# The rounding constant of the angles as a row of the angle product: three matrix products per PSUM bank in place of four

## The chip, the cores and the metric

The kernel runs on one core of a Trainium2 chip. The metric is the device time of one execution in microseconds, given as a median of several runs. Beside it stands one profiled execution, whose trace shows every instruction of the engines: TensorE (PE in the profile, its weight loads PEld), VectorE (DVE), ScalarE (ACT), GpSimd (POOL) and SyncE (SP, which here only issues transfers).

## The reference

All data are float32. `x` has 2048 positions (L) and 512 channels (D). The reference is one block of two halves, each with a layer norm whose shift, scale and gate come from `silu(c) @ w_mod`.

```python
# first half: an S4 convolution, with N = 128 states per channel
dt = exp(log_dt)[:, None];  logdA = dt * (A_re + 1j * A_im);  dB = dt * (B_re + 1j * B_im)
P = exp(logdA[:, :, None] * l[None, None, :])               # l = 0 .. L-1
K = einsum("dn,dnl,dn->dl", C_re + 1j * C_im, P, dB).real   # one filter of length L per channel
y = irfft(rfft(K, 2L) * rfft(u, 2L))[:, :L] + u * Dskip     # causal convolution, by FFT
# second half: a dense layer of 1792, mish, a dense layer back to 512
h = layernorm(x + ga * y) * (1 + cb) + sb
out = (x + ga * y) + gb * (mish(h @ w1 + b1) @ w2)
```

What matters here is `P`: for every channel and state a complex exponential, that is a decay and an angle, at every position.

## The kernel before, in words

The work falls into three stages.

The first, up to about 250 us of the span, makes the filters and their transform. Position `l` is split into a coarse and a fine part, so that the exponentials of 16 channels (`k`, one of 32 groups) are a table of 32 by 64 per state. `params` computes logarithms and angles of the parameters in four blocks `b` of 128 channels, on VectorE. They go out to DRAM (`store_pk`) and come back transposed as stationary matrices (`load_s`): `S12` for the angles, with 96 rows, of which rows 64 to 95 are ones, and `S3` for the decays. For each group `k` there are then these steps:

- `coarse` (the `pco` products and `Exp` on ScalarE) makes the decays `co`. It is done for eight groups at a time in `visit`, between two loads of ScalarE's function tables; there are four visits.
- `s_ang(k)` makes the angles in turns. It fills a pair of PSUM banks `pang` (two per tag), each by four accumulating products with the same stationary matrix `s`: the first with `ac[:, 0]` gives the angle `a`; the second, with a column of `am` broadcast over 512 columns (stride 0), adds 12582912 (MAGIC), at which float32 has steps of one, so that the bank is rounded to whole turns; the third takes MAGIC off again; the fourth, with `ac[:, 1] = -ac[:, 0]`, takes the angle off. What stays is the rounded angle less the angle.
- `s_sin(k)` reads the pair on ScalarE three times (`Abs`, two `Sin`) and fills `ec`, of which there are three buffers.
- `s_mag(k)` and `comb(k)` multiply by the decays on VectorE, in tiles `m` and `ec`.
- `s_kgen(k)` (64 small products into `pkg`), `s_ks(k)` (the copy to `ks` on ScalarE), `s_skip(k)` (VectorE), `s_ka(k)` (16 products into `pka`) and `s_tm(k)` (the copy to `gk` on ScalarE) make the filter's first transform.

The order on each engine is written out by hand: `follow` chains every instruction of PE, ScalarE, VectorE and SP behind the one before it. In step `k` PE does `s_kgen(k-1)`, `s_ang(k+3)`, `s_ka(k-3)` and, in half of the steps, the transform of a piece of the input (`u_mm`, tile `pua`); ScalarE does `s_ks(k-1)`, `u_out`, `s_sin(k+2)`, `s_tm(k-3)`; VectorE does `comb(k)` with other pieces of work between its parts: `params` of the last block, the input's statistics (`u_stats`, tile `bst`) and norm (`u_norm`, tile `x`). Three products with rows of `w_mod` (`mod_mm`, `mod_piece`) lie in single steps. The lines for PE and for the angle product are:

```python
for s in [(s_kgen, k - 1), (s_ang, k + 3), (s_ka, k - 3)] + pe.get(k, []):
    step(*s)
for s in [(s_ks, k - 1)] + se.get(k, []) + [(s_sin, k + 2), (s_tm, k - 3)]:
    step(*s)
```

The second stage, to about 345 us, multiplies the transforms and transforms back (`product`, `inverse`, tiles `pub`, `pkb`, `y`, `pz`). The third, to the end, is the norm and the two dense layers (`pm`, `po`); products that need more precision are made of three products of split operands.

## Time and profile before

| | |
|---|---|
| median of 3 runs | 718.02 us (716.53 to 719.85) |
| the profiled execution | 714.55 us, its span 712.8 us |
| mean granted TensorE clock | 0.941 of full speed |
| PE busy | 634.3 us, 89% of the span |
| DVE busy | 412.8 us, 58% |
| ACT busy | 319.9 us, 45% |
| POOL busy | 5.0 us, 1% |

Busy time is that of an engine's instructions; those of PE are pipelined and their ends are modelled, so the distance from one start to the next is the better measure there. In rows of the timeline the columns are start, duration, engine, line, operation with output and inputs, form and count; the bracket at the end is idle time just before it and what ended it. Helpers record all operations at their own lines (L147 for most products, L119 and L141 for VectorE and ScalarE), so tiles tell more than lines.

### The profile page before, as it was taken

How to read it: one execution, taken by the hardware profiler on the slowest of the kernel's cores; microseconds unless marked ns; L12 is line 12 of the kernel's file. 1: busy time of each engine (PE TensorE's matmuls, PEld its weight loads, DVE VectorE, ACT ScalarE, POOL GpSimd, SP SyncE). 2: the span in 40 equal slices, each digit the busy share in tenths (PEclk: the TensorE clock that was granted, in tenths of full speed). 3: DMA queues.
4: the chain of work that ended last, by engine and by line, in shares of the span. 5: the costliest groups of instructions: out<-in, count | busy, mean ns of one | idle time of the engine just before them, and what ended most of it. 6: DMA issues, size and time to landing. Idle time of an engine off the chain costs nothing.

```text
span 712.8 us, 11831 instructions
## 1 busy us (share of the span) xinstructions
PE 634.3 (89%) x4848; PEld 432.8 (61%) x4848; DVE 412.8 (58%) x813; ACT 319.9 (45%) x466; POOL 5.0 (1%) x12
## 2 busy tenths in 40 slices
PE   0488899889989979999249999999999999999995
PEld 0356666556656623333028778887788867888884
DVE  8889989997976657876196242342443224441113
ACT  2477798598897644543135212322132211322220
POOL 2000000000000000000000000000000000000000
PEclk9969979879969999999669999999999999999999
DMA  7842213624342479973686140052201400020002
GB/s 194 296 135 66 90 41 111 195 74 151 118 146 93 133 202 316 307 228 131 163 240 139 37 101 0 1 119 59 60 1 29 90 0 1 1 57 4 0 1 59
DMA packets 34315, 74.63 MB, mean 105 GB/s; under 512 B 5419, under 2 KB 9903, under 8 KB 33749
## 3 DMA queue, kind: packets, MB, share of 16 engines
q1 hardware_dynamic: 33380, 72.17, 34.9%
q10 hardware_dynamic: 576, 1.05, 0.7%
q8 instruction: 38, 0.62, 0.4%
q0 software_dynamic: 304, 0.66, 0.4%
q14 instruction: 17, 0.13, 0.1%
HBM read 49.73 MB, written 24.13 MB: 104 GB/s over the span
## 4 chain that ended last, share of the span: by engine, by line
PE 69%; DVE 21%; ACT 4%; DMA 3%; issue 2%; SPq 0%; ACTq 0%; DVEq 0%
PE pm L797 22%; PE po L814 22%; DVE ec L119 8%; PE pub L147 4%; PE pz L147 4%; DVE raw L119 4%; PE pkb L147 4%; PE pang L147 3%; PE pkg L147 2%; PE pka L147 2%; PE pia L762 2%; PE pco L147 2%; DVE x L119 1%; PE pua L147 1%; ACT ec L141 1%
## 5 line engine op out<-in xcount | busy, mean ns | idle before, releaser
L797 PE MATMUL pm<-hh,w1h 128*128 128x512 f32 x448 | 142.5, 398 | 0.6 <-ACT hh L119 0.6
L141 ACT ACTIVATE mh<-pm,b 128x512 f32<-128x512 f32 x56 | 38.5, 688 | 228.2 <-PE pm L797 228.2
L119 DVE TENSOR_TENSOR mal<-mh,mah 128x512 fp32r<-128x512 f32 x56 | 38.7, 691 | 155.3 <-ACT mah L119 155.0
L797 PEld LDWEIGHTS pm<-hh,w1h 128*128 128x128 f32 x448 | 84.8, 189 | 21.6 <-ACT hh L119 1.5
L814 PE MATMUL po<-w2h,mah 128*128 128x512 f32 x224 | 89.4, 399 | 0.0
L797 PE MATMUL pm<-hh,w1l 128*128 128x512 f32 x224 | 88.7, 396 | 0.0
L814 PE MATMUL po<-w2l,mah 128*128 128x512 f32 x224 | 88.6, 395 | 0.0
L814 PE MATMUL po<-w2h,mal 128*128 128x512 f32 x224 | 88.5, 395 | 0.0
L119 DVE TENSOR_TENSOR ec<-ec,co 128x1024 f32<-128x1024 f32 x64 | 75.0, 1204 | 8.4 <-ACT ec L141 8.4
L147 PE MATMUL pang<-ac,s 96*128 96x512 f32 x128 | 53.2, 461 | 25.8 <-DMA s<-pkd 25.8
L147 PEld LDWEIGHTS pkg<-ec 128*32 128x32 f32 x2048 | 35.9, 114 | 29.4 <-issue 15.4
L119 DVE TENSOR_TENSOR y<-pkb,f 128x1024 f32<-128x1024 f32 x32 | 37.7, 1220 | 27.5 <-PE pkb L147 27.5
L814 PEld LDWEIGHTS po<-w2h,mah 128*128 128x128 f32 x224 | 42.1, 188 | 14.6 <-ACT mah L119 4.9
L147 PE MATMUL pkg<-ec 128*32 128x64 f32 x2048 | 42.0, 230 | 7.6 <-DVE ec L119 6.7
L797 PEld LDWEIGHTS pm<-hh,w1l 128*128 128x128 f32 x224 | 42.3, 189 | 10.0
L814 PEld LDWEIGHTS po<-w2h,mal 128*128 128x128 f32 x224 | 42.1, 188 | 10.2
L814 PEld LDWEIGHTS po<-w2l,mah 128*128 128x128 f32 x224 | 42.1, 188 | 9.8
L147 PEld LDWEIGHTS pang<-ac,s 96*128 96x128 f32 x128 | 27.6, 215 | 32.9 <-issue 26.3
L147 PE MATMUL pang<-am,s 96*128 96x512 f32 x128 | 43.5, 425 | 0.0
L147 PE MATMUL pco<-mc,s 64*128 64x512 f32 x64 | 30.4, 624 | 11.2 <-ACT co L141 7.1
L141 ACT ACTIVATE ec<-ec,halfpi 128x1024 f32<-128x1024 f32 x32 | 37.5, 1173 | 0.0
L147 PE MATMUL pka<-bdk,ks 128*64 128x128 f32 x512 | 36.5, 288 | 0.9 <-ACT gk L119 0.9
(97 smaller groups left out, 832.2 us busy)
## 6 DMA issues: line engine op xcount, KB each, us to landing
ud<-u SPq DMA_DIRECT2D x16, 512.0 KB, 3.4
ur<-ud SPq DMA_DIRECT2D x32, 256.0 KB, 4.3
zd<-z SPq DMA_DIRECT2D x16, 512.0 KB, 3.3
zl<-zd SPq DMA_DIRECT2D x28, 256.0 KB, 4.9
x<-in_A_u SPq DMA_DIRECT2D x32, 128.0 KB, 3.0
x<-in_A_u SPq DMA_DIRECT2D x8, 512.0 KB, 6.9
out<-ot SPq DMA_DIRECT2D x32, 128.0 KB, 2.3
w1s<-in_B_w SPq DMA_DIRECT2D x8, 448.0 KB, 6.0
```

Of the source, the lines that this page charges most:

```text
L119: ins = getattr(self.engine, name)(*a, **kw)
L141: follow("act", nc.scalar.activation(out, in_, f, **kw))
L147: follow("pe", T.matmul(out, lhsT, rhs, start=start, stop=stop))
L762: T.matmul(p[64 * tl:64 * tl + 64, :], di, ZL[tt, hv][:, j % 2, tl, :], start=True, stop=True)
L797: T.matmul(p, w1[wi][:, k, fs], hh[:, hi, k, :], start=(n == 0), stop=(n == 3 * KB - 1))
L814: T.matmul(PO[tt][q], a[ai][:, P * q:P * q + P], w2[wi][:, f, :], start=(f == 0 and n == 0), stop=(f == FB - 1 and n == 2))
```

## The change

The constant MAGIC becomes row 64 of the first angle product's moving matrix. Row 64 of the stationary matrix is ones, and rows 64 to 95 of `ac[:, 0]` were zero, so the first product now gives `a + MAGIC` at once. The product that added MAGIC is gone; `am` has one column, -MAGIC. Each bank is filled by three products in place of four; all other steps stay, in the same order.

```diff
     ac = np.zeros((2, 96, 16, 32))
-    am = np.zeros((96, 2))
+    am = np.zeros((96, 1))
...
     ac[1] = -ac[0]
-    am[64] = MAGIC, -MAGIC
+    ac[0, 64] = MAGIC
+    am[64] = -MAGIC
...
-    am = gen.tile([96, 2], F32R, name="am", bufs=1)
+    am = gen.tile([96, 1], F32R, name="am", bufs=1)
...
         for e in range(2) if half is None else (half,):
-            for n in range(4):
-                rhs = ac[:, n // 3, :] if n % 3 == 0 else am[:, n - 1:n].to_broadcast([96, 512])
-                mm(PA[k][:, e, :], s[:, e, :], rhs, start=(n == 0), stop=(n == 3))
+            for n, rhs in enumerate((ac[:, 0, :], am.to_broadcast([96, 512]), ac[:, 1, :])):
+                mm(PA[k][:, e, :], s[:, e, :], rhs, start=(n == 0), stop=(n == 2))
```

## The prediction

> **What bounds the kernel now.** I read the page first: its shares, its slices, and in the list of groups the two that the change touches.

> ```profile
> PE 634.3 (89%) x4848; PEld 432.8 (61%) x4848; DVE 412.8 (58%) x813; ACT 319.9 (45%) x466; POOL 5.0 (1%) x12
> PE   0488899889989979999249999999999999999995
> DVE  8889989997976657876196242342443224441113
> PEclk9969979879969999999669999999999999999999
> L147 PE MATMUL pang<-ac,s 96*128 96x512 f32 x128 | 53.2, 461 | 25.8 <-DMA s<-pkd 25.8
> L147 PE MATMUL pang<-am,s 96*128 96x512 f32 x128 | 43.5, 425 | 0.0
> ```

> The share of 89% says little about this change, since the angle products all lie in the first third. There (slices 2 to 13) PE and DVE are both at 8 or 9 tenths, and the granted clock dips four times. So the question is, step by step, whether PE or DVE ends last. The chain of waits over 25 to 255 us answers it: its shares, all its long pieces of `pang`, and at two places what follows them.

> ```profile
> by line: DVE ec L119 23.8%; PE pang L147 8.5%; PE pkg L147 7.5%; PE pka L147 6.5%; DVE raw L119 5.9%; PE pco L147 5.4%; issue 4.7%; PE pua L147 4.4%; ACT ec L141 3.9%; DVE x L119 3.5%; DVE bst L119 2.7%; DVE m L119 2.6%; DMA pkd<-pk 2.2%; D
> ...
> 78.26 2.00 PE pang L147 x8
> 80.26 1.02 PE pka L147 x16
> 81.28 1.06 PE pua L147 x4
> ...
> 133.69 3.42 PE pang L147 x8
> 137.11 1.91 PE pka L147 x16
> 139.01 1.97 PE pua L147 x4
> ...
> 156.85 2.50 PE pang L147 x8
> 162.53 1.99 PE pang L147 x8
> 183.45 1.99 PE pang L147 x8
> 188.89 2.00 PE pang L147 x8
> 208.84 3.71 PE pang L147 x8
> 217.35 2.00 PE pang L147 x8
> ```

> A group of eight products stands for one `s_ang`. There are 32 groups (128 + 128 products in the page's list, by 8); only eight are on the chain, 19.6 us together, which is 8.5% of 230. The others lie beside VectorE.

> **What one product costs.** The starts in PE's timeline, since durations overlap: a pair of `am` products at full clock, and one at half clock.

> ```profile
> 104.46 0.60 PE L147 MATMUL pang<-am,s 96*128 96x512 f32 x2
> 104.90 0.63 PE L147 MATMUL pang<-ac,s 96*128 96x512 f32 x2
> ...
> 135.63 1.05 PE L147 MATMUL pang<-am,s 96*128 96x512 f32 x2
> 136.47 0.63 PE L147 MATMUL pang<-ac,s 96*128 96x512 f32 x1
> ```

> At full clock 104.90 - 104.46 = 0.44 us for two, 0.22 each; at half clock 136.47 - 135.63 = 0.84. Each group loses two `am` products: a group of 2.00 us becomes 1.56, one of 3.42 becomes 2.58. Their weight loads run under the products, so I count nothing more for them. [...]

> Were every group on the path, 24 at full clock and 8 taken at half would give 24 x 0.44 + 8 x 0.84 = 17.3 us: the ceiling. If VectorE hid all, 0.

> **What is on the path.** These are the rows of PE, VectorE and ScalarE at the places where the chain changes engine.

> ```profile
> 132.03 0.27 PE L147 MATMUL pkg<-ec 128*32 128x64 f32 x2 [1.90 <-DVE ec L119]
> ...
> 81.22 0.69 DVE L119 SCALAR_TENSOR_TENSOR ec<-ec,m 128x512 f32<-128x512 f32 x1
> 139.03 0.68 DVE L119 SCALAR_TENSOR_TENSOR ec<-ec,m 128x512 f32<-128x512 f32 x1
> 166.83 1.23 DVE L119 TENSOR_TENSOR ec<-ec,co 128x1024 f32<-128x1024 f32 x1 [1.71 <-ACT ec L141]
> 170.86 0.69 DVE L119 BATCH_NORM_STATS2 bst<-x 128x6 f32<-128x512 f32 x1 [1.61 <-DMA x<-in_A_u]
> 191.17 0.69 DVE L119 SCALAR_TENSOR_TENSOR ec<-ec,m 128x512 f32<-128x512 f32 x1
> 226.84 2.33 DVE L119 TENSOR_TENSOR ec<-ec,co 128x1024 f32<-128x1024 f32 x2 [0.94 <-ACT ec L141]
> 239.96 2.33 DVE L119 TENSOR_TENSOR ec<-ec,co 128x1024 f32<-128x1024 f32 x2 [0.52 <-ACT ec L141]
> ...
> 83.49 0.37 ACT L119 COPY ks<-pkg 128x256 f32<-128x256 f32 x1 [0.49 <-PE pkg L147]
> 194.12 0.37 ACT L119 COPY ks<-pkg 128x256 f32<-128x256 f32 x1 [0.48 <-PE pkg L147]
> 236.66 0.37 ACT L119 COPY ks<-pkg 128x256 f32<-128x256 f32 x1 [1.26 <-PE pkg L147]
> ```

> I go from visit to visit, because a visit is bound by ScalarE and passes on whatever the steps before it gained.

> *To the second visit.* VectorE leads until shortly before 78, then PE runs one step without a gap to the copy at 83.49, which waits for it. The group at 78.26 is in that step: 0.44. The `kgen` behind it needs VectorE's result of 81.22 + 0.69 = 81.91, and PE would come to it at 81.28 + 1.06 - 0.44 = 81.90: VectorE is just in time. ScalarE had idled 0.49 there, so it has room for 0.44 and no more.

> *To the third visit.* VectorE is without a gap and holds PE back (1.90 us of waiting at 132.03); every group up to there is hidden and only lengthens PE's waits. Then PE does the last step at half clock: the group at 133.69 gives 0.84. What is late next is VectorE's result of 139.03 + 0.68 = 139.7; PE comes to the `kgen` behind it at 139.01 + 1.97 = 140.98, less 0.84 at 140.14, still the later of the two.

> *To the fourth visit.* PE leads first: the group of 156.85, partly at half clock, gives 0.58 (two of its eight products at 0.22 to 0.42 each lie between 0.44 and 0.84; I take the low half, since the clock comes back within it), the next one 0.44. ScalarE's result at 166.83 comes by 0.58 earlier, the input that the statistics wait 1.61 us for at 170.86 by 1.02, because its load is issued when PE's `pua` frees the buffer. 1.02 is under 1.61, so it counts in full. The group at 183.45 gives nothing: the next `kgen` starts into VectorE's end. The one at 188.89 gives 0.44: VectorE was done at 191.86, the copy at 194.12 waits for PE, and its idle 0.48 covers 0.44. Sum 1.46.

> *To the end of the stage.* The groups at 208.84 (half clock, 0.84) and 217.35 (0.44) are on the chain: 1.28, and VectorE's ec at 226.84 can follow, having idled 0.94 and, before that, longer. From there the chain names VectorE; but PE has no gap, and ScalarE's copy at 236.66 waits 1.26 for PE. Three more groups lie there, 3 x 0.44 = 1.32. So this part is worth between 1.28 (VectorE leads) and 2.60 (PE leads). VectorE's idle 0.52 at 239.96 allows 1.28 + 0.52 = 1.80; I take 1.9, near that row.

> Sum: 0.44 + 0.84 + 1.46 + 1.9 = 4.64 us. Later stages have no angle products and are moved as they are: 714.55 - 4.64 = 709.91 for an execution like the profiled one. That execution is 3.47 us under the median of 718.02, so the median forecast is 718.02 - 4.64 = 713.4.

> **Edits at no cost.** The first product gets a nonzero row; it keeps its 96 rows and 512 columns and so its time. The load of `am` shrinks; its place in POOL's queue stays, and its first reader starts at 25.8 waiting for other data. No wait is added, and nothing moves past a queue. Buffers come free sooner by at most the 4.64 us, so loads of the stationary matrices start sooner by as much; they lie ahead of need and I price them at 0.

> **The clock.** Its cost is the unknown one. These are rows of busy time in stretches of 3.41 us, aligned to the steps of the granted clock (columns: stretch, length, PE, PEld, DVE, ACT, POOL, clock, DMA share, GB/s).

> ```profile
> 69.14:72.55 3.41, 2.01 (x67) 1.71 (x68) 3.41 (x7) 1.03 (x4) 0.00 (x0) 1.00 0.28 77
> 130.58:133.99 3.41, 1.72 (x66) 1.45 (x67) 3.41 (x6) 0.47 (x2) 0.00 (x0) 1.00 0.85 234
> 133.99:137.41 3.42, 3.42 (x12) 2.31 (x12) 3.42 (x6) 3.42 (x6) 0.00 (x0) 0.50 0.55 178
> 195.43:198.85 3.42, 2.10 (x20) 1.23 (x19) 3.32 (x6) 3.40 (x6) 0.00 (x0) 1.00 0.57 214
> 198.85:202.26 3.41, 2.45 (x7) 1.05 (x7) 1.02 (x2) 3.40 (x6) 0.00 (x0) 1.00 0.00 0
> 202.26:205.67 3.41, 3.41 (x7) 1.96 (x7) 3.38 (x6) 3.41 (x8) 0.00 (x0) 0.50 0.00 0
> ```

> The clock fell to half behind a stretch with PE busy 1.72, stayed full behind ones with 2.01 and 2.10, and fell behind one of 2.45. So the limit is somewhere near 1.7 to 2.4, and a stretch where PE waits for VectorE, with 0.44 less to do, comes nearer to it. [...]

> **Rivals.**

> *VectorE covers more than the chain shows.* Its slices at 8 and 9 speak for it; the waits of ScalarE for PE (0.49, 0.48) against it. Left would be the steps just ahead of the visits, at full clock, and the group at 156.85: 0.44 + 0.44 + 0.44 + 0.58 = 1.9, so 716.1.

> *The clock falls once more.* At 69 to 72, say: a step then takes PE twice as long. The rows at 133.69 and 78.26 give the price of a step: 3.42 + 1.91 + 1.97 = 7.30 us for 2.00 + 1.02 + 1.06 = 4.08; with three products per bank 6.46 for 3.64, so 2.8. 713.4 + 2.8 = 716.2.

> *Slower: the clock falls at three new places* where PE waits for VectorE. 3 x 2.8 = 8.4, less 4.64: 3.8 us over the median, 721.8. It decides from the third fall on; two give 719.0. For it speaks that 2.01 is near the limit; against it that only that one full stretch is so near.

> *More than forecast.* The clock returns one stretch of 3.41 us earlier behind a visit (behind the last it is still at half in the group of 208.84), worth 1.7, and PE leads in four more steps, 4 x 0.44: 4.64 + 3.46 = 8.1 gives 709.9; the ceiling allows it.

> **How the numbers follow.** A measurement of this kernel can tell about 0.5%, 3.6 us, from no change. Forecast, 713.4 (its own range 711 to 714.4): 0.48. More: 0.10. VectorE covers: 0.25. One fall, or two: 0.10. Three falls: 0.07. Faster by over 0.5% is the first two, 0.58; within it the next two, 0.35; slower 0.07. The range runs from 709.5, under the case of 709.9, to 718, above the two cases near 716; three falls are left out.

> **What would show it.** `pang<-am` at 64 products, a group at 1.56 us between starts; the copies at 83.5 and 194.1 waiting under 0.1 us for PE; the input's wait at 170.9 down to about 1.2 (1.61 - 1.02 + 0.58); longer waits of PE's `pkg` for VectorE between 60 and 132; stage end about 4.6 us earlier. The prediction is wrong if half-clock stretches are more, longer or fewer than before, or if those two copies come no earlier relative to the visit before them.

## The result and the profile after

The changed kernel took 712.97 us, median of 9 runs (711.97 to 716.25), beside 717.71 for the kernel before (9 runs). The ratio is 0.995, with a 95% interval of 0.9933 to 0.9968: faster by 2.3 to 4.8 us, with 4.74 between the medians. The forecast was 713.4. The profiled execution took 711.97 us, span 710.2. It lies 1.0 us under its median and the one of before 3.2 under its own, so the two traces differ by only 2.6 us, and what is read from them is an account of these 2.6.

The page after: shares, slices and groups.

```profile
PE 623.6 (88%) x4784; PEld 422.5 (59%) x4784; DVE 412.4 (58%) x813; ACT 319.9 (45%) x466; POOL 5.0 (1%) x12
PE   0388898789889989999349999999999999999995
DVE  8979989998978577866194242322443134441113
PEclk9959978979969999999679999999999999999999
L148 PE MATMUL pang<-ac,s 96*128 96x512 f32 x128 | 56.1, 485 | 27.0 <-DMA s<-pkd 26.5
```

PE lost 10.7 us of busy time and 64 products; VectorE and ScalarE do what they did. In the slices PE shows more 7s and 8s in the first third. The clock's row has the same four dips there; its slices of 17.8 us are too coarse for what follows below. The row of the `am` products in PE's view of tile `pang`, and the ends of one group in its timeline:

```profile
L148 PE MATMUL pang<-am,s x64: 377/378/629, 27.0 to 228.8; 96*128 96x512 f32 x64
...
78.86 0.50 PE L148 MATMUL pang<-ac,s 96*128 96x512 f32 x1
...
80.43 0.33 PE L148 MATMUL pka<-bdk,ks 128*64 128x128 f32 x2
```

From 78.86 to 80.43 a group takes 1.57 us, for the 2.00 of before. Its first product, with the constant in its row 64, starts 0.34 us ahead of the next (78.86, 79.20), as in the trace of before without it (104.12, 104.46). The long pieces of `pang` on the chain of waits after:

```profile
72.97 2.78 PE pang L148 x6
78.94 1.56 PE pang L148 x6
...
156.54 2.00 PE pang L148 x6
161.72 1.55 PE pang L148 x6
...
183.73 2.07 PE pang L148 x6
188.99 1.55 PE pang L148 x6
...
208.49 2.86 PE pang L148 x6
214.89 1.56 PE pang L148 x6
219.64 1.56 PE pang L148 x6
223.33 1.56 PE pang L148 x6
227.88 1.57 PE pang L148 x6
```

Two things are new. Three groups stand behind the one at 214.89, where the chain of before named VectorE: PE leads to the end. And groups stand there at half clock (72.97, 2.78 us) or partly (183.73, 2.07) that were at full clock before. The busy time by stretches of the clock, at three places between the visits where it fell and had not fallen before:

```profile
68.68:72.09 3.41, 1.32 (x52) 0.95 (x52) 3.41 (x8) 1.61 (x3) 0.00 (x0) 1.00 0.27 77
72.09:75.50 3.41, 3.41 (x41) 2.47 (x31) 3.41 (x6) 2.49 (x4) 0.00 (x0) 0.50 0.00 0
...
109.64:113.05 3.41, 1.67 (x20) 0.99 (x18) 3.41 (x6) 3.41 (x5) 0.00 (x0) 1.00 0.81 267
113.05:116.47 3.42, 2.74 (x64) 2.48 (x65) 3.42 (x7) 0.86 (x4) 0.00 (x0) 0.50 0.03 7
...
177.91:181.32 3.41, 0.91 (x14) 0.53 (x10) 3.41 (x6) 2.79 (x4) 0.00 (x0) 1.00 0.41 156
181.32:184.73 3.41, 2.95 (x65) 2.60 (x66) 3.41 (x6) 0.92 (x2) 0.00 (x0) 0.50 0.02 5
```

Ahead of each fall VectorE was busy throughout (3.41) and PE only 1.32, 1.67 and 0.91 us: PE had finished its shorter work and waited (0.9, 1.5 and 2.1 us for VectorE's `ec`, and 1.2 for ScalarE's `gk` in the first). A fourth stretch at half clock, from 140.4 to 143.8, stands beside the one that before had from 134.0 to 140.8. So the rival of the falling clock came about in this trace, three times, and the time was still as forecast. The waits of VectorE and ScalarE after:

```profile
170.36 0.69 DVE L120 BATCH_NORM_STATS2 bst<-x 128x6 f32<-128x512 f32 x1 [1.91 <-DMA x<-in_A_u]
...
232.48 0.38 ACT L120 COPY ks<-pkg 128x256 f32<-128x256 f32 x1 [0.83 <-PE pkg L148]
```

The wait for the input at 170.36 became longer (1.61 to 1.91), not shorter. The copy at 232.48 waits 0.83 us for PE, for 1.26 before. The input's load on the two chains of waits, before and after (SP's issues, then the transfer):

```profile
166.68 0.54 SPq L446
167.27 0.74 SPq L446
168.07 2.70 DMA x<-in_A_u
```

```profile
165.43 0.55 SPq L446
166.03 0.60 SPq L446
166.68 3.58 DMA x<-in_A_u
```

Counted from the third visit, the load was issued 0.94 us sooner (19.84 to 18.90), as forecast, but had landed only 0.20 sooner (23.93 to 23.73). One of its four issues took SP 1.45 us; the longest of the same four took 0.74 before.

To see where the time went, I measure from one visit to the next, at ScalarE's first table load of each (columns: start, duration, engine, line, operation, count), and to the first `pkb` product, with which the second stage is under way. Before, then after:

```profile
35.87 1.28 ACT L144 ACT_TABLE_LOAD   x1
88.20 1.28 ACT L144 ACT_TABLE_LOAD   x1
146.84 1.28 ACT L144 ACT_TABLE_LOAD   x1
198.83 1.28 ACT L144 ACT_TABLE_LOAD   x1
253.19 3.65 PE L147 MATMUL pkb<-gk,mf 128*64 128x512 f32 x16 [1.16 <-ACT f L119]
```

```profile
36.61 1.28 ACT L145 ACT_TABLE_LOAD   x1
88.52 1.28 ACT L145 ACT_TABLE_LOAD   x1
146.53 1.28 ACT L145 ACT_TABLE_LOAD   x1
198.48 1.28 ACT L145 ACT_TABLE_LOAD   x1
249.00 3.65 PE L148 MATMUL pkb<-gk,mf 128*64 128x512 f32 x16 [1.16 <-ACT f L120]
```

The same differences, in us, for all traces but that of the added work around the visits (one execution each; the experiments follow), with the time at half clock before 250 us:

| kernel | 1 to 2 | 2 to 3 | 3 to 4 | 4 to pkb | sum | half clock |
|---|---|---|---|---|---|---|
| before | 52.33 | 58.64 | 51.99 | 54.36 | 217.32 | 54.6 |
| changed | 51.91 | 58.01 | 51.95 | 50.52 | 212.39 | 64.9 |
| changed, again | 51.79 | 57.46 | 53.69 | 49.83 | 212.77 | 64.9 |
| ten groups | 51.67 | 57.46 | 52.11 | 51.70 | 212.94 | 51.2 |
| ten groups, again | 52.10 | 57.46 | 52.49 | 50.01 | 212.06 | 51.2 |
| the 22 others | 52.42 | 57.46 | 54.17 | 51.74 | 215.79 | 64.9 |
| last five | 52.50 | 57.46 | 54.38 | 51.91 | 216.25 | 51.2 |
| first five | 52.16 | 58.13 | 51.24 | 51.47 | 213.00 | 51.2 |
| five products | 54.35 | 57.47 | 54.35 | 54.16 | 220.33 | 41.0 |
| two products | 52.88 | 57.47 | 54.05 | 49.15 | 213.55 | 71.7 |
| four waits filled | 51.50 | 58.28 | 53.27 | 49.70 | 212.75 | 58.0 |
| changed, shifted | 52.38 | 57.46 | 52.33 | 51.76 | 213.93 | 68.3 |
| ten groups, shifted | 52.11 | 58.63 | 51.45 | 49.46 | 211.65 | 51.2 |

The stage of the angles became 4.93 us shorter, but the span only 2.6. The first visit came 0.74 us later in this trace. The second stage moved as it is. The last one, from the first `pm` to the start of the last long piece of `po`, took 324.08 us before (373.14 to 697.22) and 325.63 after (369.01 to 694.64), 1.55 more. The reason is at its third set of stores. VectorE's and PE's timelines there, and the issues of the stores (least, median and most ns):

```profile
L824 SPq DMA_DIRECT2D out<-ot x32: 466/562/2025, 460.7 to 706.7; - x32
...
633.75 0.69 DVE L120 TENSOR_TENSOR ot<-po,gbb 128x512 f32<-128x512 f32 x1 [3.51 <-DMA out<-ot]
...
634.50 0.50 PE L814 MATMUL po<-w2h,mah 128*128 128x512 f32 x1 [1.07 <-DVE ot L120]
```

One store took SP 2.03 us to issue (604 ns at most before). VectorE waited 3.51 us there for an earlier store of the set to land, for 1.73 at the same place before, and PE 1.07 us for VectorE.

### The profile page after: what moved, and what is told of

Same layout as the page of the kernel before. It is cut to its first block, busy times and chain, and to the rows that moved or that the text cites. A ratio compares the mean times of both kernels' runs of the same rounds, so it can differ in the third digit from the quotient of the medians.

```text
span 710.2 us, 11704 instructions
## 1 busy us (share of the span) xinstructions
PE 623.6 (88%) x4784; PEld 422.5 (59%) x4784; DVE 412.4 (58%) x813; ACT 319.9 (45%) x466; POOL 5.0 (1%) x12
## 3 DMA queue, kind: packets, MB, share of 16 engines
q10 hardware_dynamic: 576, 1.05, 0.7%
## 4 chain that ended last, share of the span: by engine, by line
PE 70%; DVE 19%; DMA 4%; ACT 4%; issue 2%; SPq 0%; DVEq 0%; ACTq 0%
PE pm L797 22%; PE po L814 21%; DVE ec L120 6%; PE pub L148 4%; PE pz L148 4%; DVE raw L120 4%; PE pkb L148 4%; PE pkg L148 3%; PE pang L148 3%; PE pka L148 2%; PE pia L762 2%; PE pco L148 2%; DVE bst L120 2%; DVE x L120 1%; PE pua L148 1%
## 5 line engine op out<-in xcount | busy, mean ns | idle before, releaser
L148 PE MATMUL pang<-ac,s 96*128 96x512 f32 x128 | 56.1, 485 | 27.0 <-DMA s<-pkd 26.5
L148 PEld LDWEIGHTS pkg<-ec 128*32 128x32 f32 x2048 | 37.8, 119 | 32.6 <-issue 15.0
L148 PE MATMUL pkg<-ec 128*32 128x64 f32 x2048 | 43.8, 239 | 12.5 <-DVE ec L120 9.9
L814 PEld LDWEIGHTS po<-w2h,mah 128*128 128x128 f32 x224 | 42.1, 188 | 16.5 <-ACT mah L120 4.9
L148 PEld LDWEIGHTS pang<-ac,s 96*128 96x128 f32 x128 | 29.1, 228 | 36.2 <-issue 27.6
L148 PE MATMUL pz<-y,mi 64*128 64x512 f32 x128 | 32.5, 626 | 4.1 <-DVE y L120 4.1
```

The costliest lines, as they stand in the source:

```text
L148: follow("pe", T.matmul(out, lhsT, rhs, start=start, stop=stop))
L814: T.matmul(PO[tt][q], a[ai][:, P * q:P * q + P], w2[wi][:, f, :], start=(f == 0 and n == 0), stop=(f == FB - 1 and n == 2))
```

## The experiments

The theories: the gain comes from the groups that the prediction put on the path (path); every removed product gains alike (spread); and the clock takes a part back where PE waits for VectorE (clock).

**Ten groups, and the 22 others.** `am` keeps a second column, of zeros, and a product with it stands in place of the removed one in some groups:

```diff
-            for n, rhs in enumerate((ac[:, 0, :], am.to_broadcast([96, 512]), ac[:, 1, :])):
-                mm(PA[k][:, e, :], s[:, e, :], rhs, start=(n == 0), stop=(n == 2))
+            zero = [am[:, 1:2].to_broadcast([96, 512])] * (0 if k in (9, 17, 19, 20, 25, 27, 28, 29, 30, 31) else 1)
+            seq = [ac[:, 0, :], *zero, am[:, 0:1].to_broadcast([96, 512]), ac[:, 1, :]]
+            for n, rhs in enumerate(seq):
+                mm(PA[k][:, e, :], s[:, e, :], rhs, start=(n == 0), stop=(n == len(seq) - 1))
```

> Three products per bank only in ten groups, those that the prediction had on the path (k = 9, 17, 19, 20, 25, 27 to 31); in the other 22 a product with a zero column stands in the place of the removed one, so PE works there as before. 20 of 64 products are gone. If the gain comes from these groups (path theory): the whole of it, about 4.6 us under the kernel before, 713.1. If every removed product gains alike because PE leads in most steps (spread theory): 20/64 of the 4.74 us measured, 1.5, so 716.2. If falls of the clock in steps where PE waits for VectorE eat a part of the changed kernel's gain (clock theory): faster than the changed kernel by one to three falls of 1 us or more, 710 to 712, and no half-clock stretch near 72, 113 and 181 us in the trace.

Measured: 0.9915 (0.9893 to 0.9937) of the kernel before, 710.95 us. 20 of the 64 products give all of the gain, so the spread theory, which asked for 0.998, falls. The trace has no fall of the clock between the visits; the stretches that answer to the first and third of those above:

```profile
69.63:73.04 3.41, 2.74 (x69) 2.42 (x70) 3.41 (x7) 1.54 (x3) 0.00 (x0) 1.00 0.10 32
73.04:76.46 3.42, 2.76 (x24) 1.29 (x22) 3.39 (x8) 2.18 (x3) 0.00 (x0) 1.00 0.00 0
...
178.86:182.27 3.41, 2.22 (x76) 1.71 (x73) 3.41 (x8) 2.48 (x4) 0.00 (x0) 1.00 0.36 136
182.27:185.69 3.42, 3.42 (x28) 2.27 (x26) 3.42 (x5) 3.42 (x5) 0.00 (x0) 1.00 0.00 0
```

The complement (`1 if k in ... else 0`):

> The complement: three products per bank in the 22 groups beside VectorE, four (one with a zero column) in the ten others. 44 of 64 products are gone. Path theory: no gain, 717.7 within 1 us. Spread theory: 44/64 of 4.74, 3.3 us, so 714.4. Clock theory: PE idles more in the steps led by VectorE and the clock falls there, so slower than before by 1 to 3 us, 718.7 to 720.7, with new half-clock stretches near 72, 113 or 181 us.

Measured: 0.9995 (0.997 to 1.0019). No gain, with 44 of 64 products gone: the path theory. Its trace has falls at 71.1, 132.6 and 180.4 us, and half clock for 64.9 us as the changed kernel has: in this pair of traces the clock fell there where the 22 groups lacked this work, and held where they had it. The clock theory's loss of 1 to 3 us did not show; the interval leaves out over 1.4 us.

**Five products, and two.** `zero` twice in every group; and the last product left out, so that the kernel lacks the fractions of the angles:

> Two products with a zero column in each bank: five products per bank, one more than before. Path theory: at least the 4.64 us of the same groups back on the other side, 722.3, and more where hidden groups come onto the path, up to the ceiling of 17.3 us. Theory that VectorE covers nearly all: 1.9 us, 719.6. Clock theory: some of it is given back, since PE waits less for VectorE and the clock falls less often, under 4 us, 718 to 721.

Measured: 1.0038 (1.0021 to 1.0056), 719.24 us: 2.7 us for 64 more products, less than the 4.64 that the path theory asked for at least. Half clock shrank to 41.0 us, and only the visits have it. By stretch the trace lost 2.02 and 2.36 us to the second and fourth visits, won 1.17 to the third, where the clock held, and 0.20 behind the last, where it was back 12 us behind the visit and not 17. So the clock gave a part back; how much of the missing 2 us this is, one trace doesn't show.

> Leaves out the last product of each bank, which takes the angle off: two products per bank, the fractional angles are missing. Path theory: a smaller second step, since ScalarE's copies had only 0.48 us of room in the steps led by PE: 1.5 to 2.5 us under the changed kernel, 710.5 to 711.5. Spread theory: another 4.7 us, 708.3. Clock theory: PE idles still more, more half-clock stretches than in the changed kernel, and no gain over it: 713 to 716.

Measured: 0.9903 (0.9871 to 0.9936), 709.62 us: 3.3 us under the changed kernel's 712.97, between the path theory's forecast and the spread theory's. The interval is 707.5 to 712.2 us on this comparison's kernel before (716.76) and holds both, so this run decides nothing between them. Half clock rose to 71.7 us. Over the four kernels with one count in every bank it goes with the products per bank: 41.0 at five, 54.6 at four, 64.9 at three, 71.7 at two.

**The changed kernel and the ten groups once more, side by side, and four waits filled.** The third has the zero product only in groups 7, 13 and 23, and two in 16:

```diff
-            zero = [...] * (0 if k in (9, 17, 19, 20, 25, 27, 28, 29, 30, 31) else 1)
+            zero = [...] * ({7: 1, 13: 1, 16: 2, 23: 1}.get(k, 0))
```

> The changed kernel once more, beside the next three on one chip. Its first measurement was 0.995 of the kernel before. Path theory with luck of the clock's phase: 0.995 again, and half-clock stretches between the visits at other places or none in this trace. Clock theory: stretches again near 72, 113, 140 and 181 us, since they follow PE's waits for VectorE, whatever the phase.

Measured: 0.9933 (0.9911 to 0.9955). Falls between the visits at 70.7, 132.2 and 179.9 us, as the clock theory said, but none at 113: the places are those of PE's waits, and which of them loses the clock varies.

> Three products per bank in the ten groups on the path, four in the 22 others, beside the changed kernel on the same chip. Clock theory: 1.5 to 3 us under the changed kernel, as 0.9915 against 0.995, and no half-clock stretch between the visits. If the difference was the chip or the draw: equal to the changed kernel within 1 us.

Measured: 0.9908 (0.9885 to 0.9931), one fall, at 131.7 us. The ten groups are 0.0025 to 0.0035 under the changed kernel in both comparisons, and 0.0030 in a third below, about 2 us, though the intervals within each comparison overlap.

> The changed kernel with a product of a zero column per bank put back in the groups k = 7, 13 and 23 and two in k = 16: those just ahead of PE's waits at 69, 112, 180 and 130 us, after which the clock fell. 54 of 64 products are gone. Clock theory: no half-clock stretch between the visits, and the time of the ten-group kernel or somewhat less, 0.991. If the ten-group kernel was faster for another reason, such as the timing of transfers: the time of the changed kernel, 0.995.

Measured: 0.9922 (0.9899 to 0.9946), between the two and not to be told from either. The filling did not do what it was meant to: falls remained at 138.8 and 183.2 us, so it doesn't test the clock theory.

The table prices the falls. The stage takes 212.4 to 213.9 us in the changed kernel's three traces (mean 213.0) and 211.7 to 212.9 in the three of the ten groups (212.2): 0.8 of the some 2 us is here, in spite of 14 to 17 us more at half clock, and what the rest is stays open. In a step that VectorE leads, PE's wait there mostly absorbed a fall. From visit 2 to 3, falls at 131.7 to 132.6 us for one stretch cost nothing: the four traces with one take 57.46. The changed kernel's first trace takes 58.01, but not for its fall at 113: VectorE leads its chain from there to 140.0, and only then does a `pkg` at half clock, in the stretch from 140.4, take 1.76 us, for 1.20 at 82.58. From visit 3 to 4, PE has 16.10 us from VectorE's `ec` to the visit where the clock held (two traces of the ten groups, and the changed kernel, shifted), 16.70 behind the fall at 181.3 and 18.33 behind that at 179.9: 0.6 us for 3.4 us at half clock, 2.2 for 6.8.

**The last five groups, and the first five.** The ten split at the last visit (`k in (27, 28, 29, 30, 31)` and `k in (9, 17, 19, 20, 25)`).

> Three products per bank only in the last five groups (k = 27 to 31, behind the last visit), four elsewhere. The prediction gave this part 1.9 us between 1.28 (VectorE leads) and 2.60 (PE leads). If PE leads to the end: 2.6 us, 0.9964 of the kernel before; if VectorE leads, 1.3 us, 0.998. If the whole gain of the ten groups (0.991) sits here, because the clock also comes back earlier: 4.3 us or more, 0.994.

Measured: 0.9957 (0.9935 to 0.998), 3.1 us. Its chain from the last visit on names all five:

```profile
210.15 2.86 PE pang L148 x6
...
217.94 1.56 PE pang L148 x6
...
222.69 1.56 PE pang L148 x6
...
226.38 1.56 PE pang L148 x6
...
230.93 1.57 PE pang L148 x6
```

The last column of the stage fell from 54.36 to 51.91 with the half-clock stretch behind the visit as long as before (13.7 us): 2.45 us, PE's bound of 2.60 and not VectorE's of 1.28. Two more traces agree in which the clock came back 16.1 to 16.5 us behind the last visit, as here, for 17.1 before: 2.66 (ten groups) and 2.60 (changed, shifted).

> The other half: three products per bank only in the groups k = 9, 17, 19, 20 and 25. The prediction gave them 0.44 + 0.84 + 1.46 = 2.74 us, 0.9962 of the kernel before. The traces of the ten-group kernel say that the first two hold and the 1.46 of the stretch before the fourth visit fails, since the input's load lands hardly earlier: 1.3 us, 0.998. If they are worthless: 1.000.

Measured: 0.9947 (0.9924 to 0.997), 3.8 us; the interval holds the forecast of 2.74 and leaves out 1.3 by little. Its trace can't confirm it: the first three columns gain 0.17 + 0.51 + 0.75 = 1.43, and the last gains 2.89 with not one product removed there, because the clock was back 10.9 us behind the visit and not 17.1. The 22 others gain 2.62 in that column in the same way (11.4 us). That is what the time of the clock's return was worth in one execution, 2.6 to 2.9 us, and one trace against one trace can't price a change below it.

**Added PE work around the visits, in the ten-group kernel.**

```diff
     def coarse(k, h):
...
+        if k >= 8:
+            mm(p, S12[2 * (k // 8) % 3][:, 2, 0, :], ac[:, 0, :])
         mm(p[:, :8 * NM], S3[k // 8][:, k % 8, :], mc[:, h, :])
...
-        for m in range(4):
+        for m in (*range(4), *(range(4) if k % 8 == 4 and k < NG - 8 else ())):
```

> The ten-group kernel with added PE work around the last three visits: the 16 pka products of the step before a visit are issued twice, and ahead of each pco product a product of 96 rows and 512 columns writes the same bank, which the pco product then overwrites. If the clock falls in the visits because PE has too little to do there, and that work keeps it up: no half-clock stretch at 90, 148 and 199 us, PE's pkg, pang, pka and pua behind them at full clock, about 1.3 us gained behind the second of them and 3 to 4 behind the last, so 4 to 5 us under the ten-group kernel. If the clock falls anyway: a pco with the added product takes 0.93 us at half clock against ScalarE's 0.50, 16 x 0.43 = 7 us per visit, 15 to 20 us slower.

Measured: 1.0322 (1.0298 to 1.0345), 741.56 us. The clock fell anyway, and stayed down for 23.9 us per visit. The first stretches, and the starts of two products in the first of them:

```profile
89.10:92.50 3.40, 3.40 (x9) 1.47 (x8) 1.92 (x3) 3.19 (x6) 0.00 (x0) 1.00 0.00 0
92.50:95.90 3.40, 3.40 (x6) 1.37 (x5) 3.40 (x6) 1.33 (x4) 0.00 (x0) 0.50 0.00 0
...
90.53 0.50 PE L148 MATMUL pco<-mc,s 64*128 64x512 f32 x1
90.96 0.49 PE L148 MATMUL pco<-ac,s 96*128 96x512 f32 x1
```

PE's row says busy for the whole of 3.40 us, and the clock fell behind it. But busy time is modelled, and the products start 0.43 us apart, where the angle products start 0.22 apart at the full clock: the eight that start in this stretch are 1.8 us of work at that rate, about half of it. So the added work did not fill PE, and this run doesn't show that a filled PE loses the clock. It shows that busy time is not the measure to forecast the clock by. What is counted stays open.

**The slow store.** In the traces of the changed kernel a load on the page's queue "q8 instruction" starts at 630.9 and 631.5 us, 2.0 and 1.8 us behind the first of those stores (628.95 and 629.65); it has 38 loads for PE's 4,848 + 4,848 instructions before, one per 255, from which I infer that they are PE's program. The five-product kernel has the same (637.9 behind 636.11) and a store issue of 1.40 us. In none of the other traces does a load start behind the first store of a set before its last; in the changed kernel's second set one started 0.27 us behind the first, and an issue took 0.99 us. To move it, eight products of data already there, in PE's wait before the dense stage:

```diff
             p = bank("pia")
+            if tt == 0 and j == 0:
+                for _ in range(8):
+                    T.matmul(p[0:64, :], di, X2[0][:, 0, :], start=True, stop=True)
```

> The changed kernel with eight more products of di and the loaded input ahead of the first pia product, in the 10 us in which PE waits for data between the second and the third stage; the pia product overwrites them. PE's instruction stream is 32 instructions longer behind that point, so that its loads on the instruction queue come about 3.5 us earlier in the dense stage and no longer within 2 us of the stores at 629 us. If the slow store there (2.03 and 1.85 us in the two traces of the changed kernel, 0.6 in the others) comes from that meeting: the longest store issue is 0.6 us, PE's wait for VectorE's ot is gone, and 1.0 to 1.5 us of the time from the first pm to the last po; 0.992 to 0.993 of the kernel before. If it belongs to the changed kernel in another way: a store issue of 1.4 us or more again, and 0.994 to 0.995. If the added work also brings the clock back sooner for the dense stage, up to 1.5 us more, to be read from the clock.

Measured: 0.9937 (0.9911 to 0.9964). The load moved to 627.5, ahead of the stores, and the slow issue is gone:

```profile
L827 SPq DMA_DIRECT2D out<-ot x32: 466/555/607, 461.8 to 706.4; - x32
```

So the meeting theory holds for the mechanism, by one run that moved the load. The time did not follow as forecast: 369.34 to 694.33 is 324.99 us, 0.6 less than 325.63, since this execution had 5.3 us at half clock behind its first `pm`, the changed kernel's 3.5. The runs can't tell 0.9937 from 0.9933 or 0.995, and the interval holds both what was expected with the meeting theory and what without.

> The same eight products added to the ten-group kernel, whose traces have no slow store. Meeting theory: nothing gained from the stores, 0.991 as without them, or a slow store if a load of PE's stream now falls on one. If the added work brings the clock back sooner: up to 1.5 us, 0.989.

Measured: 0.9907 (0.9885 to 0.9928), 709.38 us; longest issue 607 ns. Equal to the ten groups; the clock came back hardly sooner (5.5 us at half clock behind the first `pm`, for 6.3 and 6.1). The ten-group kernel, at 0.991, is the version to keep.

## Why the prediction was right, and where not

The time (713.4 for 712.97) and the direction were right, and the main cause was too: the gain sits in the ten groups named (0.9915 and 0.9908), and the other 22 are worth nothing (0.9995). Point by point the sum was less good than its total. By two of the prediction's own signs of being wrong it was: the time at half clock rose from 54.6 to 64.9 us, and the second of its two copies came only 0.04 us sooner behind its visit (47.28 to 47.24), the first 0.42.

- *To the second visit, 0.44:* 0.42, 0.54 and -0.05 in the changed kernel's three traces, 0.66, 0.23 and 0.22 with the ten groups. Right in the mean (0.34), within a scatter as large. ScalarE's copy, at 83.81, has no wait for PE left there, as said.
- *To the third visit, 0.84:* the size is of the order measured (0.63, 1.18), for the wrong reason. The stretch takes 57.46 or 57.47 us in eight traces, with two products, five products and with no edit in it (the last five groups). VectorE sets it unless the clock is at half in the last steps ahead of the visit. What the profiled execution lost there, 1.18, was its half-clock stretch at 134, and removing products doesn't reliably remove that: the third trace of the ten groups has 58.63, with half clock from 140.9.
- *To the fourth visit, 1.46:* failed; 0.04, -1.70 and -0.34, and -0.12, -0.50 and 0.54 with the ten groups. The step that failed is the input's load. In the second trace of the changed kernel PE's `pua` came 0.82 us earlier behind the visit, near the 1.02 said, but VectorE's start on the input came 23.93 us behind the visit for 24.02 before: SP's issues and the transfer took up what PE gained. The prediction moved the load as it is. In before a load of the instruction queue began 0.26 us ahead of the input's four issues (166.42, 166.68); now the issues came first, that load began 0.97 and 0.95 us behind the first of them, and one issue took 1.45 and 1.44 us. That the meeting is the cause is inferred from the traces: no run moved the load here. Then the clock fell at 181 or 179.9, in a wait of PE that the change had lengthened. In the ten groups' first two traces and the changed kernel, shifted, the clock came back 13.6 to 14.0 us behind the third visit, for 11.1 before, and held the load up instead. The 0.44 of the last group did come with the ten groups, whose time from VectorE's `ec` of that wait to the visit fell from 16.53 to 16.10.
- *To the end of the stage, 1.9 between 1.28 and 2.60:* under-sized. PE leads, 2.45 to 2.66 with the clock back nearly as late as before, and the 3.84 and 4.53 of the changed kernel hold some of the clock's return besides. I took VectorE's idle 0.52 as the limit, while PE's row had a single gap there, 0.85 us at 240.46.
- *The clock:* the falls came more often than the rival said (its place at 69 to 72 was the first), at a price under its 2.8 us: nothing, 0.6, and 2.2 for a fall of two stretches. It priced a fall at the whole step's lengthening, though in those steps PE had been waiting for VectorE. Nor does a limit in busy time hold: the clock fell behind a stretch with 3.40 us.
- *Later stages move as they are:* not quite. 1.55 us was lost in the last stage, most of it at the stores, which no step of the prediction looked at.

The forecast's total profited from errors of both signs: that it came within 0.5 us of the median is in part luck, since one of its four terms held, one had its size for another reason, one failed and one was too small. How the medians' 4.74 us divide is not shown. The pair of traces differs by 2.6: 4.93 won in the stage, 0.74 lost ahead of the first visit, 1.55 at the end.

## What to carry to other kernels

Where two engines take turns at the lead, go through the chain of waits group by group and edit only what is on it: here a third of the edit gave the whole gain, and leaving the rest alone was some 2 us better than the full edit. A share of busy time of 8 or 9 tenths on both engines didn't tell here which one led; the gaps in the timelines did: behind the last visit PE, which led, had a single one, of 0.85 us, once the clock was back. And a term worked out against one trace can be no finer than what the clock moves between two executions, here up to 2.9 us in one stretch.
